# Linear attention block on one core: x tile 2 taken off the transposing DMA and transposed on TensorE, with the crossbar blocks moved up by one tile

## The chip, the cores and the metric

The kernel runs on one core of a Trainium2 chip. The metric is device time in microseconds (us). The core's five engines run side by side: TensorE (PE; its weight loads are listed as PEld), VectorE (DVE), ScalarE (ACT), GpSimd (POOL) and SyncE (SP, which here only issues DMAs).

A run is called slow when it takes over 1.5% longer than the fastest of its kernel. Unless said otherwise, times below are fast runs. The profile of the kernel before that was at hand for the prediction is of a slow run; a fast one was taken later (experiment e1_before_again).

## The reference, cut to what matters

```python
B, S, D = x.shape                       # 1, 2048, 640; 32 heads of 20
qkv = (x @ wqkv) ...                    # wqkv is 640 x 1920
phi = lambda t: jnp.where(t > 0, t + 1, jnp.exp(t)) + 1e-6
pq, pk = phi(q), phi(k)
kv = einsum("bhsd,bhse->bhde", pk, v);  z = sum of pk over s
o = (pq @ kv) / (pq . z + 1e-6)
return o @ wo
```

All is bf16. What matters here: `x` has 2048 rows, which the kernel handles as 16 tiles of 128. To compute `x @ wk`, TensorE needs each tile transposed (`xT`), with the 640 columns in five chunks of 128.

## The kernel before

There are two ways for a tile of x into `xT`. Tiles 0 and 1 are loaded as they lie (`xn`), transposed on TensorE against an identity, and copied from PSUM to `xT` by VectorE and ScalarE. The other tiles come through DMAs that transpose on the way (the crossbar), in blocks.

```python
NPE = 2                                  # tiles transposed on TensorE
XCH = [(0, 128), (128, 256),
       (256, 512), (512, 896), (896, 1408), (1408, 2048)]

def load_xT():                           # one transposing DMA per block, SP queue
    for i, (a, b) in enumerate(XCH[NPE:]):
        P.add("sp", lambda e, a=a, b=b: e.dma_start_transpose(
            xT[...][:, :, a:b], x[0, a:b, :]), writes=[("xT", NPE + i)], dma=True)

def transpose_x(st, banks, engs):        # L197: 5 transposes; L211, L208: two copies
    for (lo, hi), b in zip(((0, 2), (2, NC_)), banks): ...
# in load_wk(), after the two halves of x tile 0:
#   x12 = x tile 1, w01 = chunk 0 of the K weights, and so on
for eng, what in (("sp", "w01 w23 w34"), ("act", "x12 w12 w45")): ...

def k_half(st, h, cs=range(NC_)):        # L281: K of one tile, 320 of 640 columns
    for c in cs:
        e.matmul(bank(b + h, HALF), xT[chunk c of tile st], wk[chunk c, half h], ...)
# ...
pool_const(); load_wk(); load_xT(); load_rest()
warm(6)                                  # matmuls on constants
transpose_x(0, (6, 7), ("dve", "act"))
warm(1)
order = "t1 k00 k10 k01 k11 k02 k12 k03 k13 k04 k14"   # t1: transposes of tile 1
...                                      # kab: tile a, chunk b, both halves
for st in range(2, NT):
    k_half(st, 0); k_half(st, 1); k_phi(st)
```

The K stage is 160 matmuls: 20 for tiles 0 and 1, ordered by weight chunk so that they can start before all of wk is there, then 10 for each further tile. After it come the attention sums, the Q stage and the output product. The change touches none of these.

## Time and profile before

| kernel before | value |
|---|---|
| time, fast runs | 100.81 us median (100.53 to 100.93) |
| the profile used for the prediction | 102.74 us, span 101.4 us, slow |
| PE busy in that profile | 97.2 us (96%) |
| x tile 1 landed / first K matmul | 5.43 / 5.98 us |
| first crossbar block (rows 256-511) landed / first read | 8.32 / 10.21 us |

A landing is the sixteenth and last increment of the DMA's semaphore; a read is the start of the first K matmul that takes the block. Both are times in the trace, from the start of the span.

First the page of that slow profile: the span, the busy times of each engine, the chain of waits that ended last (shares of the span by engine and by line), and the costliest group of the K stage.

```profile
span 101.4 us, 1793 instructions
...
PE 97.2 (96%) x694; PEld 65.4 (65%) x699; DVE 64.0 (63%) x133; ACT 45.2 (45%) x86; POOL 4.5 (4%) x17
...
PE 91%; DMA 4%; ACT 1%; issue 1%; DVE 0%
...
L281 PE MATMUL ps<-wk,xT 128*128 128x320 bf16 x160 | 23.4, 311 | 0.0
```

91% of the chain is TensorE, and the K matmuls of line 281 had no idle time before them (the last figure). Busy time of overlapping matmuls would hide small gaps, so the starts were also read one by one: from the first K matmul to the end of the stage there is no stall. The first K matmuls start 0.267 us apart (half pace below), then, from about 9.05 us, 0.136 us apart (full pace). Where the text says that the clock opens, it means this passage, read from the starts of the matmuls.

The first 12 us of the chain of waits in order of time (start, length, what):

```profile
0.79 0.42 ACT L238
1.21 0.03 issue
1.24 4.19 DMA xn<-in_x_dram
5.43 0.05 issue
5.47 0.71 PE ps L197 x5
6.19 5.81 PE ps L281 x32
```

The start waits for the load of x tile 1, then TensorE runs without a break. No transposing DMA (`xT`) is on the chain. Who TensorE's matmuls waited for, over the whole span (total us, times, longest):

```profile
PE ps L197 <- DMA xn<-in_x_dram: 1.0, 1, 1.0
PE ps L271 <- PEq L689: 0.8, 1, 0.8
PE ps L334 <- ACT w2g L464: 0.2, 1, 0.2
```

### The profile page before, as it was taken

The numbers are of one execution on the slowest core, as the hardware profiler recorded it, in microseconds if no ns is written. First come the engines' busy times: TensorE is split into PE (matmuls) and PEld (weight loads), VectorE is DVE, ScalarE is ACT, GpSimd is POOL, SyncE is SP. The second block draws the span as 40 slices with busy tenths as digits, with TensorE's granted clock in tenths as the row PEclk, the third lists the DMA queues.
The fourth block names the chain that finished last, engine by engine and source line by source line (L and its number), as shares of the span: only waits on it lengthen the run. The fifth ranks groups of instructions, "written<-read, shape, count | busy, mean of one in ns | idle before, by whom it ended". The sixth has DMA issues, their size and how long they took to land.

```text
span 101.4 us, 1793 instructions
## 1 busy us (share of the span) xinstructions
PE 97.2 (96%) x694; PEld 65.4 (65%) x699; DVE 64.0 (63%) x133; ACT 45.2 (45%) x86; POOL 4.5 (4%) x17
## 2 busy tenths in 40 slices
PE   6789999999999999999999999999999999999992
PEld 2356777777765656656677867776556677777771
DVE  2110699888884899968986500549998507955332
ACT  5110754444553044027546067577957433333222
POOL 6300000000000000000000800000000000000000
DMA  2999999999993000000000004320120233273334
GB/s 64 301 226 228 235 226 217 370 378 363 351 214 67 6 0 0 0 0 3 3 0 6 0 7 137 81 61 6 55 87 0 76 103 94 97 259 129 129 129 129
DMA packets 18372, 12.26 MB, mean 121 GB/s; under 512 B 9917, under 2 KB 18365, under 8 KB 18365
## 3 DMA queue, kind: packets, MB, share of 16 engines
q1 hardware_dynamic: 17645, 11.55, 41.7%
q10 hardware_dynamic: 720, 0.61, 1.8%
q8 instruction: 5, 0.08, 0.3%
q14 instruction: 2, 0.02, 0.1%
HBM read 5.90 MB, written 2.62 MB: 84 GB/s over the span
## 4 chain that ended last, share of the span: by engine, by line
PE 91%; DMA 4%; ACT 1%; issue 1%; DVE 0%
PE ps L281 23%; PE ps L514 22%; PE ps L334 21%; PE ps L308 17%; DMA xn<-in_x_dram 4%; PE ps L621 4%; PE ps L445 1%; PE ps L424 1%; ACT w2g L464 1%; PE ps L197 1%; PE ps L482 1%; ACT L238 0%; DVE osb L539 0%; PE ps L405 0%
## 5 line engine op out<-in xcount | busy, mean ns | idle before, releaser
L281 PE MATMUL ps<-wk,xT 128*128 128x320 bf16 x160 | 23.4, 311 | 0.0
L334 PE MATMUL ps<-xT,wqn 128*128 128x512 bf16 x95 | 22.6, 379 | 0.4 <-ACT w2g L464 0.2
L514 PE MATMUL ps<-w2p,pq 128*128 128x320 bf16 (+2 forms) x170 | 22.1, 291 | 0.0
L281 PEld LDWEIGHTS ps<-wk,xT 128*128 128x128 bf16 x160 | 16.3, 102 | 6.9
L342 ACT ACTIVATE eq<-ps 128x512 bf16<-128x512 f32 x20 | 12.0, 598 | 18.6 <-PE ps L334 18.6
L514 PEld LDWEIGHTS ps<-w2p,pq 128*128 128x128 bf16 x170 | 15.9, 98 | 6.2 <-issue 0.2
L308 PE MATMUL ps<-pk,xn 128*128 128x360 bf16 (+1 forms) x130 | 19.1, 299 | 0.0
L334 PEld LDWEIGHTS ps<-xT,wqn 128*128 128x128 bf16 x100 | 11.6, 118 | 8.1 <-ACT w2g L464 0.2
L294 ACT ACTIVATE ek<-ps 128x640 bf16<-128x640 f32 x16 | 11.2, 704 | 12.3 <-PE ps L281 11.6
L308 PEld LDWEIGHTS ps<-pk,xn 128*128 128x128 bf16 x130 | 12.6, 98 | 5.6
L507 DVE TENSOR_TENSOR pq<-pq,rd 128x512 bf16<-128x512 bf16 x20 | 7.7, 415 | 10.6 <-DMA rd<-rdc 10.6
L299 DVE SCALAR_TENSOR_TENSOR pk<-ps,ek 128x640 bf16<-128x640 f32 x16 | 13.2, 825 | 0.5
L536 ACT CAST osb<-ps 128x320 bf16<-128x320 f32 (+1 forms) x17 | 7.0, 414 | 12.8 <-PE ps L514 9.4
L539 DVE CAST osb<-ps 128x320 bf16<-128x320 f32 (+2 forms) x17 | 7.7, 462 | 6.3 <-PE ps L514 6.3
L296 DVE TENSOR_SCALAR ek<-ek 128x640 bf16<-128x640 bf16 x16 | 5.2, 324 | 6.6 <-ACT ek L294 6.6
L355 DVE TENSOR_SCALAR eq<-eq 128x512 bf16<-128x512 bf16 x20 | 5.7, 287 | 2.2 <-ACT eq L342 2.1
L346 ACT ACTIVATE rq<-ps 128x512 bf16<-128x512 f32 x11 | 6.5, 591 | 0.0
L362 DVE SCALAR_TENSOR_TENSOR pq<-ps,eq 128x512 bf16<-128x512 f32 x9 | 6.2, 692 | 0.3
L368 DVE TENSOR_TENSOR za<-pk 128x1280 f32<-128x1280 bf16 x4 | 5.8, 1484 | 0.0
L359 DVE TENSOR_TENSOR pq<-eq,rq 128x512 bf16<-128x512 bf16 x11 | 4.7, 426 | 1.1 <-ACT rq L346 0.8
L621 PE MATMUL ps<-pk,xn 128*128 128x360 bf16 (+1 forms) x30 | 4.9, 299 | 0.0
L413 POOL TENSOR_SCALAR zb<-hm,zc 128x32 bf16<-128x32 bf16 x5 | 2.1, 444 | 52.6 <-DVE zc L410 52.6
(44 smaller groups left out, 45.6 us busy)
## 6 DMA issues: line engine op xcount, KB each, us to landing
out_dram<-osb SPq DMA_DIRECT2D x15, 160.0 KB, 1.8
xn<-in_x_dram SPq DMA_DIRECT2D x2, 640.0 KB, 10.5
xn<-in_x_dram SPq DMA_DIRECT2D x1, 960.0 KB, 8.6
wqn<-in_wqkv_dram SPq DMA_DIRECT2D x1, 800.0 KB, 5.5
wv<-in_wqkv_dram SPq DMA_DIRECT2D x1, 800.0 KB, 13.7
wog<-in_wo_dram SPq DMA_DIRECT2D x1, 750.0 KB, 14.0
w2p<-w2g SPq DMA_DIRECT2D x5, 150.0 KB
rd<-rdc SPq DMA_DIRECT2D x8, 64.0 KB, 2.1
```

What stands on the lines that cost most here:

```text
L281: r = e.matmul(bank(b + h, HALF), xT[:, c * S + 128 * st:c * S + 128 * st + 128], wk[:, c * D + HALF * h:c * D + HALF * (h + 1)], start=(c ...
L294: P.add("act", lambda e: e.activation(fold(t[:, :]), two_banks(b), ACTF.Exp), reads=banks + ["table"], writes=[("ek", st % 3)])
L299: P.add("dve", lambda e: e.scalar_tensor_tensor(fold(pk[:, st * D:(st + 1) * D]), two_banks(b), 0.0, fold(t[:, :]), ALU.max, ALU.add), rea ...
L308: r = e.matmul(bank(d, PW[h]), xn[:, st * D + 128 * d:st * D + 128 * d + 128], pk[:, st * D + PO[h]:st * D + PO[h] + PW[h]], start=(st == ...
L334: r = e.matmul(bank(b), wqn[:, d * D:(d + 1) * D].rearrange("p (q c) -> p c q", c=NC_)[:, c, :], xT[:, d * S + BK * sbk:d * S + BK * (sbk ...
L342: P.add("act", lambda e: e.activation(t[:, :], bank(b), ACTF.Exp), reads=[("bank", b), "table"], writes=[("eq", i)])
L346: P.add("act", lambda e: e.activation(r[:, :], bank(b), ACTF.Relu), reads=[("bank", b), "table"], writes=[("rq", i)])
L507: P.add("dve", lambda e: e.tensor_tensor(v, v, rd[i][:, BK * h:BK * (h + 1)], ALU.mult), reads=[("rd", i, 2 * h), ("rd", i, 2 * h + 1), (" ...
L514: r = e.matmul(bank(b, hi - lo), pq[:, c * S + 128 * st:c * S + 128 * st + 128], w2p[:, c * D + lo:c * D + hi], start=(c == 0), stop=(c == ...
L536: P.add("act", lambda e: e.copy(osb[j][:, lo:hi], bank(b, hi - lo)), reads=[("bank", b)], writes=keys)
L539: P.add("dve", lambda e: e.tensor_copy(osb[j][:, lo:hi], bank(b, hi - lo)), reads=[("bank", b)], writes=keys)
L621: r = e.matmul(bank(d, PW[h]), xn[:, st * D + 128 * d:st * D + 128 * d + 128], pk[:, st * D + PO[h]:st * D + PO[h] + PW[h]], start=False, ...
```

## The change

The intent is to take pressure off the first crossbar block. Tile 2 is needed soonest of the tiles that come through it. The change loads tile 2 as it lies, right after the K weights, and transposes it on TensorE between the K matmuls of tiles 0 and 1. The first crossbar block then holds tiles 3 and 4, which are needed later. K of tile 2 is issued in two groups of chunks, since the two copies finish at different times.

```diff
-        NPE = 2
-        XCH = [(0, 128), (128, 256),
-               (256, 512), (512, 896), (896, 1408), (1408, 2048)]
+        NPE = 3
+        XCH = [(0, 128), (128, 256), (256, 384),
+               (384, 640), (640, 1024), (1024, 1536), (1536, 2048)]
...
-            for eng, what in (("sp", "w01 w23 w34"), ("act", "x12 w12 w45")):
+            for eng, what in (("sp", "w01 w23 w34 x23"), ("act", "x12 w12 w45")):
...
-            for a, b in ((2, 8), (8, 12), (12, 16)):
+            for a, b in ((3, 8), (8, 12), (12, 16)):
                 load_xn(a, b, "sp")
...
-        order = "t1 k00 k10 k01 k11 k02 k12 k03 k13 k04 k14"
+        order = "t1 k00 k10 k01 k11 k02 k12 k03 k13 t2 k04 k14"
...
-                transpose_x(st, (4, 5), ("dve", "act"))
+                transpose_x(st, *{1: ((4, 5), ("dve", "act")), 2: ((6, 7), ("dve", "act"))}[st])
...
-            k_half(st, 0)
-            k_half(st, 1)
+            for cs in ((0, 1), (2, 3, 4)) if st < 3 else (range(NC_),):
+                for h in range(2):
+                    k_half(st, h, cs)
```

## The prediction

> **What bounds the kernel now.** TensorE. The busy table gives PE 97.2 us of 101.4 (96%), and the chain of waits is 91% PE, with one DMA piece at the front: 4.19 us for x tile 1 (landed 5.43), then transposes from 5.47 and K matmuls from 5.98. Listed one by one, the K matmuls never stall before 29.2 us: the first 12 are 267 ns apart, one is 204, the rest 136. The Trainium skill ("TensorE: Matmul & The Clock Gate", Part 1) explains the step as a clock gate that opens after a sustained busy window; the trace agrees (half pace until about 9.05 us), although the clock column shows 1.00.
>
> **Was the first crossbar block late?** No. Landing of each block (DMA semaphores) against the first K matmul that reads it:
> - rows 256-511: landed 8.32, read 10.21
> - rows 512-895: landed 10.54, read about 12.9
> - rows 896-1407: landed 13.41, read about 17.0
> - rows 1408-2047: landed 16.61, read about 22.4
>
> So the change removes no wait that this trace shows. The profiled run was slow (102.74 us against 100.81 unprofiled). If the clock opened before 6 us, tile 2 would be read at about 5.98 + 20 x 0.136 = 8.7 us (estimate), barely after 8.32; a hidden stall of some tenths is possible in unprofiled runs, and the change would remove it.
>
> **What it removes, adds and moves.**
> - Adds 5 TensorE transposes inside the gapless K stream. At half pace they took 107 ns each; at full pace a 128x120 matmul with its own weight load takes 53 ns (the KV group). They stand after 16 K matmuls, after the clock opened: 5 x 0.055 = 0.28 us, all critical (estimate).
> - Adds a VectorE copy (0.29 us) and a ScalarE copy (0.48 us) before the first exp. Estimate from tile 1: 0.70 us from the second transpose's start to the first copy's finish; the reordered K steps give 0.75 to 0.8 us of cover. Stall 0 to 0.1 us. The phi chain starts up to 0.3 us later but recovers (VectorE 1.14 us per tile, TensorE 1.36).
> - Adds a 160 KB load on the SP queue (0.47 us to issue). It should land at 7.3 to 7.8 us and is read at about 9.66: no stall. The first crossbar block lands about 0.45 us later (8.8), but now serves tile 3, read near 11.8. Later blocks keep or gain slack.
> - Removes 128 rows from the crossbar (1792 to 1664, about 0.8 us of the queue's issue time) and from the later natural load. Nothing critical reads those queues before 29 us.
>
> **Sum.** +0.28 for transposes, +0.05 for copy waits, -0.05 for a possible hidden stall: about +0.3 us. Predicted 101.1 us, 8-in-10 range 100.6 to 101.6. Chances: faster by over 2% 0.02, within 2% 0.96, slower by over 2% 0.02.
>
> **What would show it.** Five more transposes about 54 ns apart after the 16th K matmul; the K stage about 0.3 us longer, from the same start near 5.98; later stages as long as before; the chain still over 90% PE; the first crossbar block landing near 8.8 without anyone waiting.
>
> **What would make it wrong.** The natural load of tile 2 landing late (after 9.6 us, or 8.2 if the clock opens early); the load slowing the last weight chunk (landed 7.11); the clock opening at another time, worth up to half of the shift; transposes at full clock costing more than a matmul of their size; the first copy holding tile 2 back; or unprofiled runs of before really stalling on the first crossbar block, which would make the change a gain of some tenths.

## The result, and the profile after

| | before | after |
|---|---|---|
| median of 5 runs, us | 100.81 (100.53 to 100.93) | 100.99 (100.84 to 101.16) |
| ratio, 95% interval | | 1.0022 (1.0001 to 1.0043) |

A ratio is the mean time of one kernel's fast runs over that of the other's fast runs of the same rounds, so it is not quite the ratio of the medians. The difference is 0.2 us, and the interval just leaves out a ratio of 1.

The profile after is of a fast run (100.98 us, span 99.4). Its span must not be set against the slow 101.4 us of before. The same lines of its page (the 621 of later lines became 622, nothing else moved):

```profile
span 99.4 us, 1806 instructions
...
PE 96.0 (97%) x699; PEld 64.8 (65%) x704; DVE 64.4 (65%) x134; ACT 45.5 (46%) x87; POOL 4.5 (5%) x17
...
PE 91%; DMA 4%; ACT 1%; issue 1%; ACTq 0%; DVE 0%
...
L281 PE MATMUL ps<-wk,xT 128*128 128x320 bf16 x160 | 22.3, 300 | 0.2 <-DMA wk<-in_wqkv_dram 0.2
```

TensorE has 699 matmuls where it had 694, and is 91% of the chain as before. The start of the chain in order of time:

```profile
1.23 0.46 ACTq L229
1.69 0.03 issue
1.72 4.02 DMA wk<-in_wqkv_dram
5.74 0.04 issue
5.79 1.80 PE ps L281 x12
7.59 0.28 PE ps L197 x5
7.87 4.21 PE ps L281 x31
```

The five new transposes stand on the chain itself with 0.28 us. The wait at the start is now for chunk 1 of wk, since x tile 1 came earlier in this run (4.28 us). TensorE's matmuls in order of time around the new transposes:

```profile
5.26 0.30 PE L281 MATMUL ps<-wk,xT 128*128 128x320 bf16 x1
5.79 1.80 PE L281 MATMUL ps<-wk,xT 128*128 128x320 bf16 x12 [0.23 <-DMA wk<-in_wqkv_dram]
7.42 0.45 PE L197 MATMUL ps<-ident,xn 128*128 128x128 bf16 x5
7.71 0.84 PE L281 MATMUL ps<-wk,xT 128*128 128x320 bf16 x5
```

And who TensorE's matmuls waited for (line 271 is the warming at the start, line 334 the Q stage):

```profile
PE ps L271 <- PEq L690: 0.8, 1, 0.8
PE ps L281 <- DMA wk<-in_wqkv_dram: 0.2, 1, 0.2
PE ps L334 <- ACT w2g L464: 0.2, 1, 0.2
```

Neither the load of tile 2 nor a crossbar block nor a copy appears. From matmul start to matmul start, the 16th and the 17th K matmul are 7.290 and 7.708 us, 0.418 apart; without the transposes they are 0.136 apart, so the five cost 0.282 us. VectorE's copy of tile 2 ran from 7.74 to 8.03 us, and tile 2's first K matmul came at 8.25.

### The profile page after: what moved, and what is told of

Its sections match the earlier page's. It is cut to its first block, busy times and chain, and to the rows that moved or that the text cites. A ratio compares the mean times of both kernels' runs of the same rounds, so it can differ in the third digit from the quotient of the medians.

```text
span 99.4 us, 1806 instructions
## 1 busy us (share of the span) xinstructions
PE 96.0 (97%) x699; PEld 64.8 (65%) x704; DVE 64.4 (65%) x134; ACT 45.5 (46%) x87; POOL 4.5 (5%) x17
## 4 chain that ended last, share of the span: by engine, by line
PE 91%; DMA 4%; ACT 1%; issue 1%; ACTq 0%; DVE 0%
PE ps L514 22%; PE ps L281 21%; PE ps L334 21%; PE ps L308 18%; PE ps L622 4%; DMA wk<-in_wqkv_dram 4%; PE ps L445 2%; PE ps L424 1%; ACT w2g L464 1%; PE ps L482 1%; ACTq L229 0%; ACT L238 0%; PE ps L197 0%; DVE osb L539 0%; PE ps L405 0%
## 5 line engine op out<-in xcount | busy, mean ns | idle before, releaser
L281 PE MATMUL ps<-wk,xT 128*128 128x320 bf16 x160 | 22.3, 300 | 0.2 <-DMA wk<-in_wqkv_dram 0.2
L281 PEld LDWEIGHTS ps<-wk,xT 128*128 128x128 bf16 x160 | 15.4, 98 | 6.5 <-DMA wk<-in_wqkv_dram 0.6
L211 DVE COPY xT<-ps 128x256 bf16<-128x256 bf16 x3 | 0.9, 291 | 5.7 <-PE ps L197 5.7
```

The source lines that it names most:

```text
L281: r = e.matmul(bank(b + h, HALF), xT[:, c * S + 128 * st:c * S + 128 * st + 128], wk[:, c * D + HALF * h:c * D + HALF * (h + 1)], start=(c ...
```

## The experiments

After the result two theories stood. Theory B, the prediction's: the change adds 0.28 us of TensorE work to a stream without gaps, and gains next to nothing. Theory A, the rival that the fast profile after suggested: with K starting near 4.8 us and the clock open early, the kernel before would need tile 2 before its block has landed, so the change removes a hidden wait of 0.3 to 0.4 us and something else costs that much.

Times are means of fast runs; those of the kernel before of the same chip were 100.81 to 100.84 us. The kernels of e8_nine to e10_filler ran on another chip than the rest. All passed the correctness test, even the two that are wrong: one wrong tile of 16 stays within its tolerance.

### e1_before_again: the kernel before once more, for a fast profile

No edit.

> The kernel before, unchanged, for a profile in the fast state. Ratio 1.000 within 0.2%. Theory A (hidden wait): K starts near 4.8 us as in the changed kernel, tile 2 is due near 7.96 us (16 matmuls of 0.136 us after 5.785) and the first crossbar block lands near 8.3, so TensorE stalls 0.3 to 0.4 us there. Theory B (no hidden wait): the block lands before 7.9 us and TensorE never stalls for it.

Measured: ratio 1.0017 (0.9979 to 1.0054). The profiled run was fast, span 99.2 us. Its chain in order of time:

```profile
1.69 0.03 issue
1.71 4.08 DMA wk<-in_wqkv_dram
5.80 0.05 issue
5.84 6.29 PE ps L281 x45
```

TensorE ran on from 5.84 us through tile 2 without a wait. The first crossbar block landed at 7.75 us and tile 2 was read at 8.03. So theory A's hidden wait was not there, but the slack was 0.28 us and no longer the 1.9 us of the slow profile. Note also the interval: a kernel against itself came out 0.17% apart, which is nearly as much as the change.

### e1b_before: one more look at it

No edit.

> One more profile of the unchanged kernel before, to see how far landings and the clock's opening move from run to run: in the fast state the first crossbar block lands within 0.2 us of the other fast profile.

Measured: one run of 100.79 us; its time is that of the fast runs. The first block landed at 8.01 us (0.25 later than in e1_before_again, a little outside the expectation) and was read at 8.27: slack 0.26 us, again no wait. Landing and read both came later here, as did x tile 1 and the K weights ahead of them; why they moved together was not tested.

### e2_after_again: the changed kernel on the same chip

No edit.

> The changed kernel, unchanged, on the same chip as the others. Both theories: 1.001 to 1.004 times before.

Measured: 101.23 us, ratio 1.0037 (1.0012 to 1.0063), with one slow run of 103.55 us left out. The 16th and 17th K matmul are 0.415 us apart (0.418 in the first profile). The load of tile 2 landed at 6.75 us and was read at 7.61.

### e3_no_wait: nothing waits for the first block at tile 2

Wrong result: K of tile 2 reads tile 0.

```diff
+            sx = 0 if st == 2 else st
-                        xT[:, c * S + 128 * st:c * S + 128 * st + 128],
+                        xT[:, c * S + 128 * sx:c * S + 128 * sx + 128],
...
-            P.add("pe", mm, reads=xT_keys(128 * st, 128 * st + 128, cs) + ...
+            P.add("pe", mm, reads=xT_keys(128 * sx, 128 * sx + 128, cs) + ...
```

> Before, with tile 2's K matmuls reading x tile 0 (wrong result on purpose), so that nothing waits for the first crossbar block at tile 2. Theory A (hidden wait): 0.3 to 0.4 us faster than before (ratio 0.996 to 0.997). Theory B (none): equal to before within 0.1 us.

Measured: 100.73 us, ratio 0.9996 (0.9958 to 1.0033), one slow run left out. The time is as theory B has it, but the interval is too wide to exclude A. The trace says more: tile 2 began at 7.87 us and the block that it would have waited for landed at 7.93. In that execution the wait would have been about 0.1 us (0.06, and the 0.05 that passed between a landing and the restart of TensorE in e6_load_only). So some runs of the kernel before may well have a hidden wait, but this one would have been of the size of the slack's scatter, not 0.3 to 0.4.

### e4_twice: the transposes of tile 2 made twice

```diff
-                    for c in range(lo, hi):
+                    for c in list(range(lo, hi)) * (2 if st == 2 else 1):
                         r = e.transpose(
```

> After, with the five transposes of tile 2 made twice. If the transposes are wholly on the critical path at full clock: 5 x 0.056 = 0.28 us slower than after (ratio to before near 1.005). If they are hidden by some other wait in after: under 0.1 us slower than after.

Measured: 101.38 us, ratio 1.0052 (1.0024 to 1.0080). In the trace the 16th and 17th K matmul are 0.694 us apart, 0.28 more than in the changed kernel. The ratio to before is the expected one, but against the changed kernel (e2_after_again) the step is 0.15 us, between the two expectations and within the scatter: undecided by time, so it was repeated larger (e8_nine).

### e5_no_transposes: the change without the five transposes

Wrong result: the two copies stay, and copy tile 0's transposes.

```diff
-                P.add("pe", mm, reads=xn_keys(st) + ["ident"], writes=[("bank", b)])
+                if st != 2:
+                    P.add("pe", mm, reads=xn_keys(st) + ["ident"], writes=[("bank", b)])
```

> After without the five transposes of tile 2 and their wait for its natural load; the two copies to xT stay and copy tile 0's transposes (wrong result on purpose). Both theories: 0.28 us faster than after plus whatever wait for the natural load there was (0.02 us in the profile), so about 0.1 us faster than before (ratio 0.999). If the early natural load or the moved crossbar blocks cost something themselves, it stays slower than that. Theory A adds: its K stage should be 0.3 to 0.4 us shorter than that of before.

Measured: 100.80 us, ratio 0.9997 (0.9959 to 1.0035); 0.43 us under e2_after_again, which ran on the same chip. With the early load, the moved blocks, the copies and the split K steps all in place but no transposes, the kernel is level with before. (The copies ran right after those of tile 1, from 5.22 and 5.71 us, and not at their place in the changed kernel.) This agrees with theory B's accounting, but the times alone cannot prove it: the runs spread from 100.35 to 101.45 us, and the interval is wider than 0.28 us. Theory A's K stage, shorter by 0.3 to 0.4 us, does not show: from first K matmul to the first matmul of the next stage it took 27.014 - 5.085 = 21.93 us, against 22.07 in e1_before_again and 21.89 in e1b_before.

### e6_load_only: the early load of tile 2 alone

```diff
-            for eng, what in (("sp", "w01 w23 w34"), ("act", "x12 w12 w45")):
+            for eng, what in (("sp", "w01 w23 w34 x23"), ("act", "x12 w12 w45")):
...
-            for a, b in ((2, 8), (8, 12), (12, 16)):
+            for a, b in ((3, 8), (8, 12), (12, 16)):
```

> Before plus the early natural load of tile 2 alone; the crossbar blocks and tile 2's route stay. Theory A (hidden wait for the first block): the block lands about 0.45 us later, so 0.4 us slower than before (ratio 1.004). Theory B (no hidden wait, slack in the first block): equal to before within 0.1 us.

Measured: 101.22 us, ratio 1.0036 (1.0009 to 1.0063): 0.4 us slower, the number that theory A gave. The block, which still brings tile 2, landed at 8.62 us, 0.6 to 0.9 later than in the two profiles of before that are not slow, and its landing is now on the chain:

```profile
3.13 5.49 DMA xT<-in_x_dram
8.62 0.05 issue
8.66 5.47 PE ps L281 x39
```

TensorE's matmuls in order of time show the wait:

```profile
6.80 1.25 PE L281 MATMUL ps<-wk,xT 128*128 128x320 bf16 x8
8.66 1.12 PE L281 MATMUL ps<-wk,xT 128*128 128x320 bf16 x7 [0.61 <-DMA xT<-in_x_dram]
```

The view takes the modelled ends of overlapping matmuls and gives 0.61 us; by starts it is 0.77. How large the delay is on average takes more than this run. The first block has 256 rows in all kernels but e7 and e9. It landed at 8.42 us in the mean of the six profiles with the early load (after, e2, e4, e5, e6, e8), and at 7.97 in the mean of the four without it that are not slow (e1, e1b, e3, e10): 0.46 us later, and the latest of all in this run. Issuing the load holds back the block's own issue by 0.47 us (from 2.65 to 3.13 us), which is enough for that. The Trainium skill ("DMA: Bandwidth & Descriptors", section "Issuing engines are not separate DMA queues") says that all DMAs run on the same 16 engines and interleave; a delay by the load's 160 KB on shared engines is thus possible too, but no run here shows it. Theory B's expectation for this run fell: it took the slack of the first block for larger than the delay, and 0.26 to 0.28 us of slack does not cover 0.46. By these means about 0.2 us of wait was due; the measured 0.4 has an interval of 0.1 to 0.6. In the full change the same block landed at 8.60 and 8.27 us in two profiles, but served tile 3, read at 9.61 and 9.79. Giving it tiles 3 and 4 is thus what makes room for the load.

### e7_small_first: the changed block sizes alone

Tile 2 has a crossbar block of its own; nothing is transposed on TensorE for it.

```diff
-               (256, 512), (512, 896), (896, 1408), (1408, 2048)]
+               (256, 384), (384, 640), (640, 1024), (1024, 1536), (1536, 2048)]
```

> Before with the changed kernel's block sizes, tile 2 in a crossbar block of its own (128 rows), no transposes added. Theory A: the smaller first block lands about 0.8 us earlier (7.5 us), the hidden wait goes, 0.3 us faster than before (ratio 0.997). Theory B: equal to before within 0.1 us.

Measured: 100.74 us, ratio 0.9980 (0.9955 to 1.0004). That lies between the theories and proves neither. In the trace the small block landed at 7.81 us (K weights came late in that run, chunk 4 at 7.13 against 6.44 in e1_before_again) and tile 2 was read at 8.67, so there was no wait in it to remove. The same small block landed at 7.18 us in e9_chunk_order.

### e8_nine: the transposes of tile 2 made nine times

As e4_twice, with 9 in place of 2.

> After, with the five transposes of tile 2 made nine times (40 more; same result). If each is wholly on the critical path at the full clock: 40 x 0.056 = 2.24 us slower than after, 2.5 us slower than before (ratio near 1.025), and the K stage from the 17th K matmul on as long as before. Rival (TensorE has slack that takes them up, or transposes let the clock fall): clearly under 2 us, or clearly over 2.5 us with K matmuls 0.267 us apart.

Measured: 103.27 us (six fast runs), ratio 1.0245 (1.0217 to 1.0272): 2.44 us over before, for 45 transposes more than before. That is 54 ns each, end to end (49 to 61 by the interval). The trace, TensorE's matmuls in order of time:

```profile
6.79 0.98 PE L281 MATMUL ps<-wk,xT 128*128 128x320 bf16 x6
7.61 2.68 PE L197 MATMUL ps<-ident,xn 128*128 128x128 bf16 x45
10.12 1.11 PE L281 MATMUL ps<-wk,xT 128*128 128x320 bf16 x7
```

By starts, 45 transposes put 2.51 us between two K matmuls, 56 ns each. The K matmuls after them go on 0.136 us apart, so TensorE did not fall back to half pace. Within the interval, every transpose reaches the end of the kernel in full. Scaled to five it is 0.27 to 0.28 us, as the trace of the changed kernel has it.

### e9_chunk_order: chunk 2 of wk before chunk 1

On the small blocks of e7_small_first, an attempt at a faster start.

```diff
-        order = "t1 k00 k10 k01 k11 k02 k12 k03 k13 k04 k14"
+        order = "t1 k00 k10 k02 k12 k01 k11 k03 k13 k04 k14"
```

> Before with the smaller crossbar blocks of the earlier experiment and chunk 2 of wk used before chunk 1, because chunk 2 landed 0.1 to 0.4 us earlier in every fast profile but one. If the wait for chunk 1 at the fifth K matmul is what the start loses: 0.1 to 0.3 us faster than before (ratio 0.997 to 0.999). If the clock's opening is: no change.

Measured: 100.99 us, ratio 1.0018 (0.9983 to 1.0052): no gain, so the expectation's first branch missed; its second, no change, fits but is not shown by this. (The landings that it starts from were read loosely: chunk 2 came 0.19 to 0.26 us before chunk 1 in seven of the nine profiles taken till then that are not slow, and 0.58 and 0.77 before it in e1b_before and e4_twice.) Its profiled run had the shortest span of all profiled runs (98.8 us, wait for the chunk down to 0.11 us), and its other five runs took up to 101.44. One good profile was not the kernel's mean.

### e10_filler: one more warming matmul

```diff
-        warm(1)
+        warm(2)
```

> Before with one more warming matmul after tile 0's transposes, to fill TensorE's idle time before x tile 1 lands. If that idle time is what delays the clock: K matmuls at 0.136 us from the start, and no run over 101.5 us; 0 to 0.3 us faster. Rival: the clock opens at its own time whatever the filler, and the filler delays tile 1's transposes: 0 to 0.3 us slower.

Measured: 100.87 us, ratio 1.0005 (0.9977 to 1.0033). The first three K matmuls still came 0.27 and 0.23 us apart before full pace, and tile 1's transposes began at 4.72 us though its load had landed at 4.40. No run was over 101.14, but neither was one of the kernel before over 101.19 in those rounds. It helps nothing that can be measured here, and the first theory falls for this run: filling the gap did not give full pace from the start. The trace's own record has the clock open at 5.71 us, later than in seven of the eight other traces that have such a record, all without the filler.

### Where the scatter comes from

Times in us, from the traces. The 1st, 16th, 17th and 21st K matmul start, then what passes from the 21st to the 160th:

```
                     1st    16th   17th    21st   21st to 160th
before (slow)       5.98    9.53   9.66   10.21   18.88
e1_before_again     4.97    7.35   7.49    8.03   18.88
e1b_before          5.40    7.59   7.73    8.27   18.88
after               4.82    7.29   7.71    8.25   18.88
e2_after_again      5.09    7.47   7.89    8.43   18.88
e5_no_transposes    5.09    7.32   7.46    8.00   18.88
e7_small_first      5.32    7.99   8.13    8.67   18.88
e8_nine             4.80    7.47  10.12   10.66   18.88
```

From the first matmul of the next stage to the last matmul of the kernel it is 69.94 us in all of these, and in the rest (where the last column is 18.88 to 18.89). So every profiled run differs from the others only before the 21st K matmul: in when x tile 1 and the weight chunks land, in when TensorE passes from 0.267 to 0.136 us per matmul, and in what the edit puts there (transposes, or the wait of e6_load_only). That holds for the slow profile too: the 2.2 us that it is longer than e1_before_again all lie there, in a first K matmul that comes 1.0 us later and in half pace until 9.05 us. The 16th K matmul, which the change does not touch, lay at 6.99 to 7.99 us in the twelve profiles that are not slow. In the six with the early load of tile 2 (after, e2, e4, e5, e6, e8) its mean is 7.42, in the others (e1, e1b, e3, e7, e9, e10) 7.47. The early load does not slow the start by anything that shows above that scatter.

## Why the prediction was right

It said 101.1 us, +0.3 us, and got 100.99 us, +0.2 us (and +0.4 in e2_after_again). Its two small terms, +0.05 for copies and -0.05 for a hidden wait, cancel, so the total tests only the 0.28 us of the transposes. Point by point:

- **TensorE is the limit and has no gaps.** Right: every transpose that was added came out at the end, 2.44 us for 45 of them.
- **Five transposes cost 5 x 0.055 = 0.28 us.** Right: 0.282 and 0.279 us by matmul starts in the two profiles of after, and the kernel without them is level with before within its scatter. The prediction took the figure from 128x120 matmuls at full clock. The 275 ns that the Trainium skill has for a transpose in a kernel ("TensorE: Matmul & The Clock Gate", Part 4) are a duration; five of them in a row would have given 1.4 us (estimate).
- **Copies: 0 to 0.1 us of stall.** It was 0: the copy was done 0.22 us before tile 2's K matmul.
- **No wait on the first crossbar block; a hidden one of at most some tenths, weighed at 0.05 us.** Right in size. In two profiles of before that are not slow there was none, nor in e10_filler, which loads tile 2 the same way (0.21 us of slack); in the execution of e3_no_wait it would have been about 0.1 us. The intervals of e3, e5 and e7 leave room for an average wait of some tenths.
- **The early load costs nothing.** Right for the whole change, but the margin was mis-sized. The prediction said landed at 7.3 to 7.8, "read at about 9.66". In the fast profile it landed at 7.37 and was read at 7.42, with 0.05 us to spare; in e2_after_again 0.86 was left. That nothing waited in the first of these was partly luck. The slow profile's half pace to 9.05 us had made the reads look late. The prediction named the possibility, late "after 9.6 us, or 8.2 if the clock opens early", but even its 8.2 took the slow profile's first K matmul at 5.98 us; in the fast one it was 4.82.
- **The first crossbar block lands about 0.45 us later and nobody waits.** It landed at 8.60 us against a predicted 8.8, with 1.0 us of slack before tile 3. The delay was right: 0.46 us between the means of the profiles with and without the early load (see e6_load_only, itself the latest of them). The 8.8 was late because it started from the slow profile's 8.32.
- **Later stages as long as before.** Right to 0.01 us.

What stays open: how many unprofiled runs of the kernel before wait at tile 2, and for how long. The slack in profiles was 0.28 and 0.26 us in before, 0.21 in e10_filler, and a missing 0.06 us in e3_no_wait. The times cannot tell, since scatter between runs is larger than such a wait.

Where did the gain go, then? The change bought slack: the first crossbar block has 1.0 us where it had 0.28. It paid 0.28 us of TensorE time for it, and in a stream that, as far as the profiles show, was hardly waiting on that block, slack is worth next to nothing.

## What to carry to other kernels

Before moving work onto the engine that is the limit, look for the wait which the move removes, by setting the landing of each transfer against its first read; where there is slack, even little, the move costs its full length, as it did here. Do that in more than one profile: here a slow profile showed 1.9 us of slack where fast ones had 0.28. When an effect is below the scatter between runs, multiply the suspected cost (nine times the transposes) and read its slope, rather than time it once more.

## What the Trainium skill lacked or had wrong

- "TensorE: Matmul & The Clock Gate", Part 4, gives a duration of about 275 ns for a transpose in a kernel and says that the full clock does not engage for transposes. Here transposes in a K stream at full pace started 56 ns apart (five and 45 in a row), with a modelled duration of 219 ns each; at half pace, where K matmuls took 0.267 us, they started 107 ns apart, with about 311 ns. So they ran at the pace of the matmuls around them, and what one adds to a stream is the 56 ns, not its duration. Whether transposes alone would keep the clock open was not tested for longer than 2.5 us (e8_nine).
- The same page has the clock open after a busy window of about 3.4 us that does not start with the kernel. The runs agree. The packed traces of nine runs hold clock records: the clock is full from 4.10 us (e9_chunk_order) to 5.78 us (e2_after_again) on, though the first matmul starts at 0.82 us in all. It stays full for 95.573 us in eight of them and 98.987 us in e8_nine, 28 and 29 times 3.413 us. In the four traces without records the starts of the matmuls give the opening: 5.5 to 6.6 us in e4, e5 and e7, 9.05 in the slow profile.
- It lacks how much idle time in such a window is forgiven. An estimate with the page's 3.4 us: in the slow profile an earlier window ended near 5.6 us, TensorE idled for 1.2 us of it (4.30 to 5.47), and the clock did not open; in e7_small_first the window to 6.6 us had 0.5 us of idle time (4.29 to 4.81), and it did. In e1b_before the clock had opened at 4.15 us, and 0.8 us of idle time after that (4.30 to 5.11) did not close it.
- The same page warns that clock events in a trace can be unreliable. Here those that exist could be relied on: where the starts show the passage in the K matmuls (e1_before_again, e2_after_again, e6_load_only, e10_filler), the record lies within 0.02 us of it. But four traces hold none, the slow one among them, and the profile's mean clock reads 1.00 everywhere, half pace included.
- "DMA: Bandwidth & Descriptors" has a figure for the issue of a transposing DMA for small tiles only. Here the first block held the SP queue 1.3 us for 128 rows of 640 and 1.7 to 2.3 us for 256 rows; a second block of 384 rows held it 2.2 to 3.2 us. A plain load of 128 rows held it 0.43 us.
